# Two attentions and a routed mixture of experts on one core: logits in one block, the last tile emptied by two engines, a new order in the first two beats

## The chip, the cores and the metric

The kernel runs on one core of a Trainium2 chip. Its engines work side by side, each through its own queue in order: TensorE (PE; its weight loads are listed as PEld), VectorE (DVE), ScalarE (ACT), GpSimd (POOL), and SyncE (SP), which here issues nearly all DMA transfers. The metric is the device time of one execution in microseconds (us); smaller is better.

## The reference

```python
def sm_attn(qq, kk, vv):
    s = scale * np.matmul(qq, kk.transpose(0, 1, 3, 2))
    a = np.exp(s - np.max(s, axis=-1, keepdims=True))
    a = a / (np.sum(a, axis=-1, keepdims=True) + 1e-09)
    return np.matmul(a, vv)
p_packed = sm_attn(p, k, v)             # p: (8, 8, 32, 64); q, k, v: (8, 8, 576, 64)
out = sm_attn(q, p_packed, p_packed)    # attention back from the 32 packed rows
...
x = attn_out.transpose(0, 2, 1, 3).reshape(4608, 512)
logits = x @ w_gate                     # 8 experts
e_idx = np.argmax(logits, axis=1)
gate_w = softmax(logits)[row, e_idx]
eom = 1.0 / (1.0 + np.exp(-(x @ w_output_gate)))
for e in range(E):                      # only rows whose expert is e
    h = np.maximum(x[mask] @ w1[e], 0.0)        # 512 -> 1024
    out[mask] = gate_w[mask, None] * eom[mask, e, None] * (h @ w2[e])
```

## The kernel before

The eight batches are eight **beats**. A beat is the mixture of experts of one batch, `ffn(b)`: for each of two halves of its 576 rows (256 and 320) eight up-projections `ps_h` (6 matmuls each, since both factors are split into a high and a low part, `ah`/`al` and `Gh`/`Gl`), each followed by a relu on ACT and the remainder of the split on DVE, both into `hT`; and then the products `ps_o` with `w2h`/`w2l`, tile by tile of 128 rows (`L565`; the short last tile at `L580`), each scaled into `ob` and stored. One expert is guessed per batch (`estar`, from the mean of the packed rows), all rows go through that one, and rows that chose another are put right at the end (`leftover`).

`ffn` yields after each piece: 1 to 8 are the up-projections of the first half, 9 to 16 its products, 17 to 24 and 25 to 35 those of the second half. At yield i the characters of `PLANS[b]` behind `i:` each emit one more piece of other work, and this order is the order of every engine's queue (it is written by hand; no planner moves anything):

- `y` is the next piece of `encode` for the next batch (scores `ps_s`, maxima, exponentials, transposes `ps_a1T`, their copies `a1T`, product `ps_pp`, transpose `ps_ppT`, gate projections `ps_pg`, copied to `pg`, the guess `ps_e`/`e_top`/`estar`); `x` the same for the batch after it
- `t` is the next piece of `route` for the batch of this beat, `r` for the next batch (scores `ps_s2T`, softmax on DVE and ACT, transposed attention `a2T`, its parts `ah` and `al`, the logits, `gate`, the count `ps_cnt`, and last the update of `keys`)
- `W`/`w` weights (loads from the guessed expert's address, then casts `w2h` and remainders `w2l`), `G`/`g` the products `ps_G` of the packed rows with `w1` and their parts `Gh`/`Gl`, `k`, `v`, `q` loads, `d` delayed stores

`START` is the same for what comes before beat 0; a digit in it emits matmuls on zeros, `keep_warm`, as many as `CFG["warm"]` says. PSUM has 8 banks, four with the tag "a" (attention) and four with "f" (up-projections, products, logits, count). A piece that needs a bank waits in its engine's queue for the last reader of the bank's earlier content; a tile of SBUF is waited for in the same way (`ob` has four buffers).

The logits: `a2T` holds the transposed attention, 576 columns for each of NG = 2 halves of the features. Stationary is `pg`, the 16 gate columns written twice beside each other (32 columns); the four blocks of 128 columns of `a2T` go to four groups of 32 PSUM partitions, side by side, and the remaining 64 columns to the bank's columns 128 to 191. Both parts are copied by ACT, transposed by PE, and copied by DVE into `L`.

The last tile of the last beat (tile 3 of batch 7) is computed in two halves of 256 columns in two banks; DVE empties the first while PE computes the second, which ACT empties.

Of the kernel before, what the change touches and what calls it, by code (L numbers as in the profile page):

```python
# [18 lines left out]

P = 128  # L20
BANK = 512
CFG = dict(raw=6, rq=2, pa=4, w1=4, wst=4, w2=6, a1T=2, at=2, row=2, ht=4, ob=4, last=(4, 2, 3), warm=(8, 2, 2, 2, 2, 0, 5),
           pool=("w1.0", "w1.1", "w1.2", "w1.3", "w2.0", "w2.1", "w2.2", "w2.3", "w3.3", "w4.3", "w5.3", "w6.3", "w7.3",
                 "sub0.0.1", "al0.0.1"))


# [2 lines left out]
START = "kkvvqqkkYYYY1YY2YYY3YY4YYtYYWtttWYtttttttty6GGvvqqkkvv"  # L29
BESIDE = "8:ry 9:yrr 10:yrrrt 11:yr 12:wrr 13:wrqq 14:rkk 15:r "  # L30
REST = "16:xr 17:x 18:r 19:xvv 20:x 22:x 24:x 25:xxw 26:ww 27:rw 28:r 30:r 31:rxg 32:xg 33:gw 34:ww"
PLANS = ["2:GG 4:WW 6:W 8:WW 9:tt 10:tWW 11:yy 12:Wyy 13:tt 14:ttty 15:ty 16:tyy 17:ty 19:yt 20:y 21:ryyr 22:yr 23:y "
# [3 lines left out]
         "1:y 2:y 4:yWW 5:y 7:yy 8:ry 9:rry 10:rrry 11:ryw 12:rrw 13:rqq 14:rkkt 15:r " + REST] \  # L36
        + ["0:yW 1:y " + BESIDE + REST] * 3 \
        + ["0:yW 1:y " + BESIDE + REST.replace("16:xr", "20:r"), "0:W 8:l 18:l 20:lt 22:l 23:l 24:l 25:l 27:l 28:l 30:l"]
# [3 lines left out]
def tile_packed_attn_then_moe(ctx, tc, qT, kT, v, pT, w_go, w1, w2, out):  # L42
# [82 lines left out]
    wgo = const.tile([P, NPAIR, 2 * E], F32, name="wgo")  # L125
    L = const.tile([P, T, 2 * E], F32, name="L")
    nc.gpsimd.memset(L[REM:, TF], 0.0)
    oh = const.tile([P, T, E], F32, name="oh")
    nc.gpsimd.memset(oh[REM:, TF], 0.0)

# [81 lines left out]
    def encode(b):  # L212
# [87 lines left out]
        ps_g = [bank("ps_pg", "f" if b else "a")[:, :2 * E] for _ in range(NG)]  # L300
        by_head(ps_g, ppT, [wgo[:, c] for c in range(NPAIR)])
        yield
        R[b] = pg = sb.tile([P, NG, 2, 2 * E], F32, tag="pg", name="pg", bufs=3)
        for g in range(NG):
            nc.vector.tensor_copy(pg[:, g], ps_g[g].rearrange("p (i e) -> p i e", i=1).to_broadcast([P, 2, 2 * E]))
        yield
        if b:
            yield from guess(pg[:, :, 0, 0:E])

    def route(b):  # L310

        ah = sb.tile([P, NG, S], F32R, tag="ah", name="ah", bufs=CFG["at"], **WIDE)
        al = sb.tile([P, NG, S], F32R, tag="al", name="al", bufs=CFG["at"], **WIDE)
        A[b] = (ah, al)

        s2 = [scores(b, packed[b], pairs("q", b, hf), "s2T", "a" if b else "f") for hf in range(2)]
        yield
        both = sb.tile([P, NG, 2, HS], F32, tag="row", name="s2", bufs=CFG["row"])
        rows = [both[:, g] for g in range(NG)]

        def turn(hf):
            for g in range(NG):
                nc.vector.transpose(rows[g][:, hf], s2[hf][g])

        turn(0)
        yield
        if b:
            turn(1)
            yield
        for part in ([0, 1],) if b else ([0], [1]):  # L330
            ts = slice(part[0] * HS, (part[-1] + 1) * HS)
            n = (ts.stop - ts.start) // NP
            sf = [x.rearrange("p a b -> p (a b)")[:, ts] for x in rows]
            sv = [x.rearrange("p (j n) -> p j n", n=NP) for x in sf]
            sms = []
            for g in range(NG):
                mx = sb.tile([P, S // NP, 1], F32, tag="mx", name="mx", bufs=2)[:, :n]
                nc.vector.tensor_reduce(mx, sv[g], axis=AX.X, op=ALU.max)
                eng("sub", b, part[0], g).tensor_tensor(sv[g], sv[g], mx.to_broadcast([P, n, NP]), ALU.subtract)  # L339
                yield  # L340
            for g in range(NG):
                nc.scalar.activation(sf[g], sf[g], AF.Exp, scale=QK)  # L342
            yield
            if part == [0]:
                turn(1)
                yield
            for g in range(NG):
                sm = sb.tile([P, S // NP, 1], F32, tag="sm2", name="sm2", bufs=2)[:, :n]
                nc.vector.tensor_reduce(sm, sv[g], axis=AX.X, op=ALU.add)
                nc.vector.tensor_scalar_add(sm, sm, 1e-9)  # L350
                nc.vector.reciprocal(sm, sm)
                sms.append(sm)
                yield
            for g in range(NG):
                eng("mul", b, part[0], g).tensor_tensor(sv[g], sv[g], sms[g].to_broadcast([P, n, NP]), ALU.mult)
                nc.vector.transpose(a2T[:, g, ts], sf[g])  # L356
                if ts.stop == S:
                    nc.sync.dma_start(a2_d[b * T:(b + 1) * T, :, g].rearrange("t p n -> p t n"),
                                      a2T[:, g].rearrange("p (t n) -> p t n", n=P))
                yield  # L360
            for g in range(NG):
                nc.scalar.copy(ah[:, g, ts], a2T[:, g, ts])  # L362
            yield
            for g in range(NG):
                eng("al", b, part[0], g).tensor_tensor(al[:, g, ts], a2T[:, g, ts], f(ah[:, g, ts]), ALU.subtract)  # L365
            yield
        lgs = sb.tile([P, P + REM], F32, tag="row", name="lgs", bufs=CFG["row"])
        lg = bank("ps_lg", "f")
        pgs = R.pop(b).rearrange("p g i e -> p g (i e)")
        beside([lg[t_ * 4 * E:(t_ + 1) * 4 * E, :P] for t_ in range(TF)],  # L370
               [[(pgs[:, g], a2T[:, g, t_ * P:(t_ + 1) * P]) for g in range(NG)] for t_ in range(TF)])
        matmuls(lg[:4 * E, P:P + REM], [(pgs[:, g], a2T[:, g, SF:S]) for g in range(NG)])
        yield
        nc.scalar.copy(lgs[:, :P], lg[:, :P])
        nc.scalar.copy(lgs[:4 * E, P:], lg[:4 * E, P:P + REM])
        yield
        lT = bank("ps_lgT", "f")
        nc.tensor.transpose(lT[:, :P], lgs[:, :P], ident)
        nc.tensor.transpose(lT[:REM, P:P + 4 * E], lgs[:4 * E, P:], ident[:4 * E, :4 * E])
        yield  # L380
        nc.vector.tensor_copy(L[:, :TF], lT[:, :P].rearrange("p (t i e) -> p t i e", i=2, e=2 * E)[:, :, 0])
        nc.vector.tensor_copy(L[:REM, TF], lT[:REM, P:P + 2 * E])
        yield from gate(b)

    def gate(b):
# [152 lines left out]
    def store():  # L538

        while keep:  # L540
            b, t_, cs, ob, ps, sc, by_dve = keep.pop(0)
            if b < 2 and t_ < 2:
                nc.scalar.activation(ob, ob, AF.Copy, scale=sc)
            elif by_dve:
                nc.vector.tensor_scalar_mul(ob[:, cs], ps[:, cs], sc)
            else:
                nc.scalar.activation(ob[:, cs], ps[:, cs], AF.Copy, scale=sc)  # L547
            nc.sync.dma_start(out[b * S + t_ * P:b * S + (t_ + 1) * P, cs], ob[:, cs])

    def product_out(b, t_, c0, hs):  # L550
        w2s = W[b][1]
# [4 lines left out]
        sc = scm_all[:r, b, t_:t_ + 1]  # L556
        if t_ < TF:
            lo = 640 - 2 * P + c
            parts = 2 if (b, t_) == (B - 1, CFG["last"][-1]) else 1
            for x in range(parts):  # L560
                cs = slice(x * DM // parts, (x + 1) * DM // parts)
                ps = bank("ps_o", "f") if x else ps
                for fc in range(FC):
                    for i, (a, m) in enumerate(three((hs[fc][:, c:c + P], hs[fc][:, lo:lo + P]), w2s[fc])):
                        nc.tensor.matmul(ps[:, cs], a, m[:, cs], start=fc == i == 0, stop=fc == FC - 1 and i == 2)  # L565
                    if fc % 2 and (fc < FC - 1):
                        yield
                keep.append((b, t_, cs, ob, ps, sc, parts > 1 and x == 0))
                if b > 1 or t_ > 1:
                    store()  # L570
                else:
                    nc.scalar.copy(ob, ps)
        else:
            seq = []
            for fc in range(FC):
                wh, wl = w2s[fc]
                both, one = (hs[fc][:, c:c + 2 * r], wh, 2 * r), (hs[fc][:, c:c + r], wl, r)
                seq += [one, both] if fc == FC - 1 else [both, one]
            for i, (a, m, n) in enumerate(seq):
                nc.tensor.matmul(ps[:n], a, m, start=i == 0, stop=i == len(seq) - 1)  # L580
                if i % 6 == 5:
                    yield
            low = sb.tile([r, DM], F32, tag="ob", name="low", bufs=CFG["ob"])
            nc.scalar.copy(low, ps[r:2 * r])
            nc.vector.tensor_tensor(ob[:r], ps[:r], low, ALU.add)
            nc.vector.tensor_scalar_mul(ob[:r], ob[:r], sc)
            nc.sync.dma_start(out[b * S + SF:(b + 1) * S], ob[:r])
# [254 lines left out]
```

## Time and profile before

| | us |
|---|---|
| three runs | 416.25, 416.55, 418.04; median 416.55 |
| profiled execution | 416.11 |
| its span, first to last instruction | 414.3 |
| PE busy in the span | 399.4 |
| DVE, ACT, POOL busy | 282.4, 181.7, 41.1 |

The span is what the trace shows; the 1.8 us around it belong to the execution and are in no row. Busy time overlaps between engines; only waits of the engine that the others wait for lengthen the span.

### The profile page before, as it was taken

Reading aid. Unit: us, or ns where it says so; the run is one execution under the profiler, and the core shown is the slowest. Engines: PE = TensorE matmul, PEld = TensorE weight load, DVE = VectorE, ACT = ScalarE, POOL = GpSimd, SP = SyncE. Lnnn points to the kernel's source line nnn. Section 1 sums busy time; section 2 is a strip of 40 time slices with the busy share of each in tenths; the row PEclk is TensorE's granted clock in tenths of the full one; section 3 lists DMA queues with packets and bytes.
Section 4 is the critical chain, followed back from the end, with each engine's and each line's share of the span. In section 5 each row is a group of like instructions: output and inputs, shape, how many; then the busy total and the mean of one; then the engine's idle time right before and its main releaser. Section 6 shows DMA issues by size and latency. Waiting matters only on the chain.

```text
span 414.3 us, 9584 instructions
## 1 busy us (share of the span) xinstructions
PE 399.4 (96%) x3696; PEld 321.1 (78%) x3696; DVE 282.4 (68%) x817; ACT 181.7 (44%) x411; POOL 41.1 (10%) x36
## 2 busy tenths in 40 slices
PE   6899999899999999999999999999999999999994
PEld 4658876677768888788977888788877888798873
DVE  2669588684886876749774786749774795758620
ACT  2356425562467337442645337351645335532310
POOL 6010000360024200020002000020002000010010
PEclk9999999999999999999999999999999999999998
DMA  7899329930797089602992079701960058102911
GB/s 243 320 375 411 112 61 367 394 126 33 251 404 266 9 271 411 247 27 102 347 412 90 6 229 405 295 27 65 357 226 34 27 196 326 38 27 87 366 30 53
DMA packets 36687, 83.61 MB, mean 202 GB/s; under 512 B 3614, under 2 KB 16288, under 8 KB 36640
## 3 DMA queue, kind: packets, MB, share of 16 engines
q1 hardware_dynamic: 36608, 82.98, 54.2%
q8 instruction: 30, 0.49, 0.5%
q14 instruction: 17, 0.14, 0.1%
q0 software_dynamic: 32, 0.00, 0.0%
HBM read 67.76 MB, written 15.27 MB: 200 GB/s over the span
## 4 chain that ended last, share of the span: by engine, by line
PE 78%; DVE 1%; ACT 1%; issue 0%
PE ps_o L565 38%; PE ps_h L85 21%; PE ps_o L580 6%; PE ps_G L92 3%; PE ps_pp L92 2%; PE ps_s L92 2%; PE ps_s2T L92 2%; PE ps_a1T L240 1%; PE ps_lg L92 1%; ACT hT L523 1%; PE ps_lh L685 0%; PE ps_lo L685 0%; ACT a L231 0%; DVE Gl L77 0%; PE ps_lg L85 0%; DVE al L365 0%
## 5 line engine op out<-in xcount | busy, mean ns | idle before, releaser
L565 PE MATMUL ps_o<-w2h,hT 128*128 128x512 f32 (+1 forms) x528 | 168.5, 391 | 0.0
L565 PEld LDWEIGHTS ps_o<-w2h,hT 128*128 128x128 f32 x528 | 98.2, 188 | 25.8 <-ACT Gh L76 5.0
L526 DVE SCALAR_TENSOR_TENSOR hT<-ps_h,hT 128x256 fp32r<-128x256 f32 x192 | 61.0, 352 | 59.9 <-ACT hT L523 59.3
L565 PE MATMUL ps_o<-w2l,hT 128*128 128x512 f32 (+1 forms) x264 | 101.4, 384 | 0.0
L85 PE MATMUL ps_h<-ah,Gh 128*128 128x256 f32 (+1 forms) x256 | 78.3, 306 | 1.7 <-DVE hT L526 0.5
L85 PE MATMUL ps_h<-ah,Gl 128*128 128x256 f32 (+1 forms) x256 | 75.8, 296 | 0.0
L85 PE MATMUL ps_h<-al,Gh 128*128 128x256 f32 (+1 forms) x256 | 75.7, 296 | 0.0
L523 ACT ACTIVATE hT<-ps_h 128x320 fp32r<-128x320 f32 (+1 forms) x128 | 51.3, 414 | 43.4 <-PE ps_h L85 42.3
L463 POOL TENSOR_TENSOR w2l<-wst,w2h 128x1024 fp32r<-128x1024 f32 x13 | 31.2, 2407 | 308.6 <-ACT w2h L461 278.7
L565 PEld LDWEIGHTS ps_o<-w2l,hT 128*128 128x128 f32 x264 | 49.7, 188 | 8.6
L85 PEld LDWEIGHTS ps_h<-ah,Gh 128*128 128x128 f32 x256 | 48.5, 189 | 6.2 <-issue 1.8
L85 PEld LDWEIGHTS ps_h<-al,Gh 128*128 128x128 f32 x256 | 48.6, 190 | 0.2
L85 PEld LDWEIGHTS ps_h<-ah,Gl 128*128 128x128 f32 x256 | 48.5, 190 | 0.2 <-DVE Gl L77 0.2
L547 ACT ACTIVATE ob<-ps_o,scm_all 128x512 f32<-128x512 f32 (+1 forms) x28 | 19.0, 680 | 39.7 <-PE ps_o L565 37.1
L461 ACT CAST w2h<-wst 128x1024 fp32r<-128x1024 f32 x32 | 33.4, 1069 | 3.3 <-PE ps_o L565 2.8
L77 DVE TENSOR_TENSOR Gl<-ps_G,Gh 128x512 fp32r<-128x512 f32 (+1 forms) x36 | 20.5, 624 | 10.5 <-ACT Gh L76 10.3
L463 DVE TENSOR_TENSOR w2l<-wst,w2h 128x1024 fp32r<-128x1024 f32 x19 | 23.2, 1220 | 6.2 <-ACT w2h L461 6.2
L362 ACT CAST ah<-a2T 128x576 fp32r<-128x576 f32 (+1 forms) x18 | 11.2, 620 | 33.7 <-DVE a2T L356 33.7
L580 PE MATMUL ps_o<-w2h,hT 128*128 128x512 f32 x64 | 25.7, 401 | 0.1
L342 ACT ACTIVATE s<-s 128x576 f32<-128x576 f32 (+1 forms) x18 | 11.1, 629 | 29.8 <-DVE s L339 29.2
L580 PE MATMUL ps_o<-w2l,hT 128*64 128x512 f32 x64 | 23.9, 393 | 0.0
L76 ACT CAST Gh<-ps_G 128x512 fp32r<-128x512 f32 (+1 forms) x36 | 17.1, 548 | 9.4 <-PE ps_G L92 8.9
(182 smaller groups left out, 440.7 us busy)
## 6 DMA issues: line engine op xcount, KB each, us to landing
w<-in_w_dram SPq DMA_DIRECT2D x36, 512.0 KB, 5.7
wst<-in_w_dram SPq DMA_DIRECT2D x36, 512.0 KB, 8.7
vt<-in_v_dram SPq DMA_DIRECT2D x16, 640.0 KB, 9.0
k<-in_kT_dram SPq DMA_DIRECT2D x14, 576.0 KB, 10.5
q<-in_qT_dram SPq DMA_DIRECT2D x14, 576.0 KB, 10.2
out_dram<-ob SPq DMA_DIRECT2D x31, 256.0 KB, 3.3
a_d<-a2T SPq DMA_DIRECT2D x16, 320.0 KB, 8.0
out_dram<-ob SPq DMA_DIRECT2D x10, 128.0 KB, 5.3
```

The costliest lines, as they stand in the source:

```text
L76: (hi_eng or nc.scalar.copy)(hi, src)
L77: (lo_eng or nc.vector).tensor_tensor(lo, src, f(hi), ALU.subtract)
L85: res = nc.tensor.matmul(dst, a, m, start=j == 0, stop=j == len(seq) - 1)
L92: res = nc.tensor.matmul(dst, a, m, start=j == 0, stop=j == len(seqs[0]) - 1)
L362: nc.scalar.copy(ah[:, g, ts], a2T[:, g, ts])
L461: nc.scalar.copy(hi, st)
L463: eng("w", b, j).tensor_tensor(lo, st, f(hi), ALU.subtract)
L523: nc.scalar.activation(hT[:, :n], ps, AF.Relu)
L526: nc.vector.scalar_tensor_tensor(hT[:, d0:d0 + s1 - s0], ps[:, s0:s1], 0.0, f(hT[:, s0:s1]), op0=ALU.max, op1=ALU.subtract)
L547: nc.scalar.activation(ob[:, cs], ps[:, cs], AF.Copy, scale=sc)
L565: nc.tensor.matmul(ps[:, cs], a, m[:, cs], start=fc == i == 0, stop=fc == FC - 1 and i == 2)
L580: nc.tensor.matmul(ps[:n], a, m, start=i == 0, stop=i == len(seq) - 1)
```

## The change

The gate columns of a batch now lie between blocks of zeros in one of three tiles `pgs`, cleared once at the start, so that a window of 32 columns has them above or below 16 zero columns. The four blocks use one window; the 64 remaining columns use the other and are added into the second 16 partitions of the first group. One 128x128 copy and one transpose then do for all five. The last tile is computed in one bank over its full width; DVE scales its left half and ACT its right half, and SP and ACT each issue one store. The remainder `w1.3` (fourth chunk of w2 of batch 1) is no longer on POOL's list and is done by DVE. Two counts of `warm` are smaller. In `PLANS[0]` and `PLANS[1]` pieces stand at other places; their number is the same.

```diff
-CFG = dict(..., warm=(8, 2, 2, 2, 2, 0, 5),
-           pool=("w1.0", "w1.1", "w1.2", "w1.3", "w2.0", ...
+CFG = dict(..., warm=(5, 2, 2, 2, 2, 0, 4),
+           pool=("w1.0", "w1.1", "w1.2", "w2.0", ...
...
-PLANS = ["2:GG 4:WW 6:W 8:WW 9:tt 10:tWW 11:yy 12:Wyy 13:tt 14:ttty 15:ty 16:tyy 17:ty 19:yt 20:y 21:ryyr 22:yr 23:y "
-         "24:wt 25:wkkrr 26:tr 27:trr 28:drqq 29:r 30:t 31:g 32:gr 33:rg",
-         "0:ytWW 1:t 2:yWW 3:t 4:yWW 5:vv 6:y 7:y 8:ytWW 9:yytt 10:y 11:y 12:yd 13:y 14:ry 15:rry 16:yrr 17:ryw 18:w 19:qq 20:kk 21:r 22:r "
-         "24:rx 25:rx 26:rx 27:rxt 28:rxvv 29:rw 30:rw 31:grww 32:g 33:grrw 34:xw",
+PLANS = ["2:GG 4:WW 6:W 8:WW 9:tt 10:tWW 11:yy 12:Wyy 13:tt 14:yyttt 15:t 16:tyy 17:ty 19:yt 20:y 21:ryyr 22:yyr "
+         "24:wt 25:wkkrr 26:tr 27:rr 28:drqq 29:r 31:g 32:gr 33:rg 35:tt",
+         "0:tWW 1:t 2:yWW 3:ty 4:yWW 5:vv 6:y 7:y 8:ytW 9:yyW 10:yyt 11:yy 12:ryd 13:yrr 14:yyrr 15:w 16:r 17:tw 18:t 19:qq 20:kk 21:r 22:r "
+         "24:rx 25:rx 26:rx 27:rx 28:rxvv 29:rw 30:rw 31:grww 32:g 33:grrw 34:xw",
...
+    pgs = [const.tile([P, 2 * NG + 1, 2 * E], F32, name=f"pg{i}") for i in range(3)]
+    for pg in pgs:
+        nc.gpsimd.memset(pg, 0.0)
...
-        R[b] = pg = sb.tile([P, NG, 2, 2 * E], F32, tag="pg", name="pg", bufs=3)
+        R[b] = pg = pgs[b % 3]
         for g in range(NG):
-            nc.vector.tensor_copy(pg[:, g], ps_g[g].rearrange("p (i e) -> p i e", i=1).to_broadcast([P, 2, 2 * E]))
+            nc.vector.tensor_copy(pg[:, 2 * g + 1], ps_g[g])
...
-        lgs = sb.tile([P, P + REM], F32, tag="row", name="lgs", bufs=CFG["row"])
+        lgs = sb.tile([P, P], F32, tag="row", name="lgs", bufs=CFG["row"])
         lg = bank("ps_lg", "f")
-        pgs = R.pop(b).rearrange("p g i e -> p g (i e)")
-        beside([lg[t_ * 4 * E:(t_ + 1) * 4 * E, :P] for t_ in range(TF)],
-               [[(pgs[:, g], a2T[:, g, t_ * P:(t_ + 1) * P]) for g in range(NG)] for t_ in range(TF)])
-        matmuls(lg[:4 * E, P:P + REM], [(pgs[:, g], a2T[:, g, SF:S]) for g in range(NG)])
-        yield
-        nc.scalar.copy(lgs[:, :P], lg[:, :P])
-        nc.scalar.copy(lgs[:4 * E, P:], lg[:4 * E, P:P + REM])
+        pg = R.pop(b).rearrange("p i e -> p (i e)")
+        for g in range(NG):
+            up, down = slice(4 * E * g, 4 * E * (g + 1)), slice(4 * E * g + 2 * E, 4 * E * (g + 1) + 2 * E)
+            for t_ in range(TF):
+                nc.tensor.matmul(lg[t_ * 4 * E:(t_ + 1) * 4 * E, :P], pg[:, down], a2T[:, g, t_ * P:(t_ + 1) * P],
+                                 start=g == 0, stop=g == NG - 1 and t_ > 0)
+            nc.tensor.matmul(lg[:4 * E, :REM], pg[:, up], a2T[:, g, SF:S], start=False, stop=g == NG - 1)
+        yield
+        nc.scalar.copy(lgs, lg[:, :P])
         yield
         lT = bank("ps_lgT", "f")
-        nc.tensor.transpose(lT[:, :P], lgs[:, :P], ident)
-        nc.tensor.transpose(lT[:REM, P:P + 4 * E], lgs[:4 * E, P:], ident[:4 * E, :4 * E])
-        yield
-        nc.vector.tensor_copy(L[:, :TF], lT[:, :P].rearrange("p (t i e) -> p t i e", i=2, e=2 * E)[:, :, 0])
-        nc.vector.tensor_copy(L[:REM, TF], lT[:REM, P:P + 2 * E])
+        nc.tensor.transpose(lT[:, :P], lgs, ident)
+        yield
+        lv = lT[:, :P].rearrange("p (t i e) -> p t i e", i=2, e=2 * E)
+        nc.vector.tensor_copy(L[:, :TF], lv[:, :, 0])
+        nc.vector.tensor_copy(L[:REM, TF], lv[:REM, 0, 1])
...
-            parts = 2 if (b, t_) == (B - 1, CFG["last"][-1]) else 1
-            for x in range(parts):
-                cs = slice(x * DM // parts, (x + 1) * DM // parts)
-                ps = bank("ps_o", "f") if x else ps
...
+            if (b, t_) == (B - 1, CFG["last"][-1]):
+                rows = out[b * S + t_ * P:b * S + (t_ + 1) * P]
+                l, r_ = slice(0, DM // 2), slice(DM // 2, DM)
+                nc.vector.tensor_scalar_mul(ob[:, l], ps[:, l], sc)
+                nc.scalar.activation(ob[:, r_], ps[:, r_], AF.Copy, scale=sc)
+                nc.sync.dma_start(rows[:, l], ob[:, l])
+                nc.scalar.dma_start(rows[:, r_], ob[:, r_])
+            else:
+                keep.append((b, t_, ob, ps, sc))
```

## Rows read from the trace of the kernel before

**Rows 1.** Windows: us, busy us (instructions) by engine, granted PE clock, DMA share, GB/s.
```profile
0.00:20.00 20.00, 14.92 (x238) 10.39 (x238) 8.75 (x32) 5.21 (x14) 7.59 (x20) 1.00 0.80 277
...
66.89:69.20 2.31, 2.31 (x34) 0.59 (x33) 2.21 (x6) 2.17 (x4) 0.00 (x0) 1.00 1.03 420
...
74.87:78.79 3.92, 2.73 (x53) 1.18 (x52) 2.45 (x4) 1.62 (x2) 0.35 (x1) 1.00 1.07 397
...
178.76:225.80 47.04, 47.04 (x438) 38.54 (x437) 33.45 (x95) 22.14 (x50) 2.45 (x2) 1.00 0.57 211
```

**Rows 2.** Chain that ended last, in steady beats: start us, us, what.
```profile
197.06 1.13 PE ps_s L92 x32
198.19 0.57 PE ps_lg L92 x16
198.76 0.20 PE ps_lg L85 x4
...
210.99 0.15 PE ps_lgT L379
...
218.14 1.88 PE ps_G L92 x32
...
225.80 5.75 PE ps_h L85 x48
```

**Rows 3.** The same chain at the end of beat 0 and start of beat 1.
```profile
72.53 0.21 DVE g_cnt L430
...
73.59 1.20 DVE Gl L77 x2
74.79 1.33 DVE al L365 x2
...
76.77 1.31 PE ps_s L92 x16
```

**Rows 4.** Timeline of PE in beat 0: start us, us; idle before, releaser.
```profile
40.83 1.03 PE L240 MATMUL ps_a1T<-ident,a 128*128 128x128 f32 x8
...
46.03 0.65 PE L92 MATMUL ps_pp<-vt,a1T 128*32 128x64 f32 x32 [0.50 <-ACT a1T L246]
```

**Rows 5.** Timeline of DVE and SP's queue in beat 0, around the guess.
```profile
56.01 0.84 DVE L323 STREAM_TRANSPOSE s<-ps_s2T 128x288 f32<-128x288 f32 x2
...
57.22 0.15 DVE L290 COPY e_top<-ps_e 128x8 f32<-128x8 f32 x1
...
58.93 2.59 SPq L447 DMA_DIRECT2D w<-in_w_dram  x4
```

**Rows 6.** Timeline of ACT at the start of beat 1.
```profile
76.74 0.69 ACT L547 ACTIVATE ob<-ps_o,scm_all 128x512 f32<-128x512 f32 x1 [2.54 <-DMA out_dram<-ob]
77.33 1.04 ACT L461 CAST w2h<-wst 128x1024 fp32r<-128x1024 f32 x1
79.80 0.39 ACT L523 ACTIVATE hT<-ps_h 128x256 fp32r<-128x256 f32 x1 [1.44 <-PE ps_h L85]
```

**Rows 7.** DMA issues from 64 to 80 us: KB each, median us to landing.
```profile
out_dram<-ob SPq DMA_DIRECT2D x4, 256.0 KB, 7.5
```

**Rows 8.** Timeline of PE in the second half of beat 1.
```profile
103.97 0.39 PE L85 MATMUL ps_h<-ah,Gh 128*128 128x320 f32 x1 [0.33 <-DVE e_top L290]
```

**Rows 9.** Chain that ended last, in the last beat.
```profile
369.14 10.91 PE ps_o L565 x48
...
398.04 10.09 PE ps_o L565 x66
```

**Rows 10.** Timeline of DVE and ACT on the last tile.
```profile
405.28 0.48 DVE L545 TENSOR_SCALAR ob<-ps_o,scm_all 128x256 f32<-128x256 f32 x1 [6.82 <-PE ps_o L565]
...
408.15 0.47 ACT L547 ACTIVATE ob<-ps_o,scm_all 128x256 f32<-128x256 f32 x1 [5.01 <-PE ps_o L565]
```

**Rows 11.** Timeline of PE in the first microseconds.
```profile
1.12 3.78 PE L114 MATMUL warm<-blank 128*128 128x128 f32 x16 [1.12 <-DVE blank L106]
...
7.51 1.40 PE L92 MATMUL ps_s<-k,pt 64*32 64x288 f32 x16 [0.91 <-DMA k<-in_kT_dram]
```

More of the change, by code (lines that the diff above doesn't have):

```diff
@@ L21 @@
 BANK = 512
-CFG = dict(raw=6, rq=2, pa=4, w1=4, wst=4, w2=6, a1T=2, at=2, row=2, ht=4, ob=4, last=(4, 2, 3), warm=(8, 2, 2, 2, 2, 0, 5),
-           pool=("w1.0", "w1.1", "w1.2", "w1.3", "w2.0", "w2.1", "w2.2", "w2.3", "w3.3", "w4.3", "w5.3", "w6.3", "w7.3",
+CFG = dict(raw=6, rq=2, pa=4, w1=4, wst=4, w2=6, a1T=2, at=2, row=2, ht=4, ob=4, last=(4, 2, 3), warm=(5, 2, 2, 2, 2, 0, 4),
+           pool=("w1.0", "w1.1", "w1.2", "w2.0", "w2.1", "w2.2", "w2.3", "w3.3", "w4.3", "w5.3", "w6.3", "w7.3",
                  "sub0.0.1", "al0.0.1"))
@@ L302, in encode @@
         yield
-        R[b] = pg = sb.tile([P, NG, 2, 2 * E], F32, tag="pg", name="pg", bufs=3)
+        R[b] = pg = pgs[b % 3]
         for g in range(NG):
-            nc.vector.tensor_copy(pg[:, g], ps_g[g].rearrange("p (i e) -> p i e", i=1).to_broadcast([P, 2, 2 * E]))
+            nc.vector.tensor_copy(pg[:, 2 * g + 1], ps_g[g])
         yield
         if b:
-            yield from guess(pg[:, :, 0, 0:E])
+            yield from guess(pg[:, 1::2, 0:E])
     def route(b):
@@ L540, in store @@
         while keep:
[L541 to L548, printed above, removed]
+            b, t_, ob, ps, sc = keep.pop(0)
+            nc.scalar.activation(ob, ob if b < 2 and t_ < 2 else ps, AF.Copy, scale=sc)
+            nc.sync.dma_start(out[b * S + t_ * P:b * S + (t_ + 1) * P], ob)
     def product_out(b, t_, c0, hs):
@@ L558, in product_out @@
             lo = 640 - 2 * P + c
-            parts = 2 if (b, t_) == (B - 1, CFG["last"][-1]) else 1
-            for x in range(parts):
-                cs = slice(x * DM // parts, (x + 1) * DM // parts)
-                ps = bank("ps_o", "f") if x else ps
[L563 to L566, printed above, removed]
-                        yield
-                keep.append((b, t_, cs, ob, ps, sc, parts > 1 and x == 0))
+            for fc in range(FC):
+                for i, (a, m) in enumerate(three((hs[fc][:, c:c + P], hs[fc][:, lo:lo + P]), w2s[fc])):
+                    nc.tensor.matmul(ps, a, m, start=fc == i == 0, stop=fc == FC - 1 and i == 2)
+                if fc % 2 and (fc < FC - 1):
+                    yield
[8 more added lines that the diff above has]
+                keep.append((b, t_, ob, ps, sc))
                 if b > 1 or t_ > 1:
```

## The prediction

> **What bounds the kernel now.** I read the windows by stage first: in a steady beat the reader should see TensorE (PE) busy for every one of its 47.04 us [rows 1]. There, time is PE work and nothing else: an edit is worth the PE instructions that it takes away, and edits to DVE, ACT or POOL are worth nothing. Next I read the chain that ended last. In a steady beat it is one unbroken run of PE pieces, which gives the price of each piece when nothing waits [rows 2]; about the start of beat 1 it leaves PE, and the reader should see DVE pieces, and then a PE piece that costs more than in a steady beat [rows 3]. PE is late only in the first two beats, so what their new plan is worth is read from the waits there: rows 4 to 8. The last beat ends in one tile, its emptying and its store [rows 9, 10]; the first microseconds have filler matmuls [rows 11].
>
> **The change part by part.** The sum is made against the profiled execution, 416.11 us (span 414.3 and 1.8 around it); the median of the three runs is 416.55, 0.44 above it.
>
> *Logits.* Removed on PE: the second transpose, 0.15 in each beat [rows 2]. In beats 2 to 7 it lies on the path: 6 x 0.15 = 0.9 us off. (Beats 0 and 1 are counted with their waits below.) The logit matmuls stay ten instructions, recorded as 16 and 4; they took 0.57 + 0.20 = 0.77 [rows 2], four column groups side by side and then the remainder in the first group. Now the remainder follows each half, still in the first group, whose own work is unchanged. I take 0. Bounds: 0.20 less a beat if the remainder hides beside the other groups, 0.20 more if its return to the first group stops the queue: 8 x 0.20 = 1.6 either way. ACT loses a 32x64 copy and DVE writes smaller pg copies: hidden behind PE in a steady beat, 0. The three memsets are POOL work long before anything reads pg: 0.
>
> *Beat 0.* The a1T copies (the second y of 14) move ahead of the steps that write ah. The transposes that they copy ended by 41.9, yet PE stood 0.50 before ps_pp for these copies [rows 4], because they were behind the ah casts in ACT's queue. Moved up they fall where ACT waited for a2T: 0.5 off, bounds 0 and 0.5. What they pass, ah and al of the second half, is read only by the matmuls after ps_pp. Then the guess of the expert (y at 22, not 23) passes the second turn of the scores on DVE: it starts at 56.01 rather than 57.22, 1.2 us earlier, and with it the weight loads that wait for it in SP's queue [rows 5]. The turn and the hT pieces behind it come 1.0 later; what reads them last in that half is PE work still to come. The first reader of these weights, ps_G, took 2.31 us [rows 1] against 1.88 in a steady beat [rows 2]: 0.4 off if it waited for the loads. With the transpose: 0.5 + 0.4 + 0.15 = 1.05 off.
>
> *Start of beat 1.* Three edits meet here. The keys update (the last t, 73.59 - 72.53 = 1.06 us of DVE) goes behind Gl and al [rows 3]. The scores of batch 2 go behind two up-projections, so they no longer stand in PE's queue waiting for the banks that Gl frees. Logits and up-projection thereby move ahead of them. The stretch from 74.87 to 78.79 is 3.92 us [rows 1]; its work is ps_s 1.13 and logits 0.77 [rows 2], so 2.0 us is waiting. DVE's al then ends at 74.79 + 1.33 - 1.06 = 75.1, less what beat 0 gave, just as PE has finished the logits: the 2.0 can all go.
> What is late next is ACT. Its scaling of the last tile of beat 0 waited until 76.74 for a store that frees its buffer, and a 1.04 us cast and the first relu are queued behind it [rows 6]. That cost nothing, since PE came late anyway; after the cast ACT even stood idle 1.44. Now PE wants a bank for its fourth up-projection at 74.87 - 1.05 + 0.77 + 3 x 0.72 + 1.13 = 77.9 (0.72 is 5.75 / 8 [rows 2]), and the logit copy that frees it is done 0.69 + 1.04 + 0.39 and its own time, about 2.3, after the wait ends. If the store lands 1.2 earlier, as the loads ahead of it do, that is 77.8: no wait. If it lands as before, it is 79.0; and ACT's work up to the exponentials that the a1T transposes need then ends only 1.4 (its idle time) earlier, while PE comes 1.05 + 2.0 = 3.05 earlier: 1.7 given back. Bounds 0 and 1.7; I take 0.6, nearer to the first since the store, 7.5 us to landing [rows 7], queues behind those loads: 2.0 - 0.6 = 1.4 off.
>
> *Rest of beat 1.* The guess and the softmax of batch 2 move into DVE's gap ahead of the second half, and PE's wait of 0.33 for e_top goes [rows 8]. But the exponentials (r at 16) now stand before the first relu of that half on ACT, and count and keys come at 17 and 18, 1.06 us of DVE between two hT pieces. I take 0.2 off; bounds 0.5 off, 0.5 on. The fourth w2l of batch 1 goes from POOL to DVE, and is ready before PE's product comes to it: 0.
>
> *End.* 48 full-width records take 10.91, 0.227 each; the last 66, of which 18 are full and 48 of half width, take 10.09 [rows 9]. So the halved tile costs 10.09 - 18 x 0.227 = 6.0, and in one run 24 x 0.227 = 5.45: 0.55 off; I take 0.3, as the short runs about the last beat's leftover pieces are slower. Then both halves of one bank are read. Side by side that is one 0.48, as now; one after the other 0.48 + 0.47 [rows 10]. No row shows two engines in one bank at once; the nearest, relu on ACT and remainder on DVE of ps_h, run in turn. I take in turn: 0.47 - 0.3 = 0.2 on; bounds 0.5 off and 0.5 on, for the second queue's store too.
> [...]
>
> *Filler matmuls.* Three fewer at the start, one fewer later. The first eight end at 4.9, and the scores after them wait for k [rows 11]: 0.
>
> Sum: -0.9 - 1.05 - 1.4 - 0.2 + 0.2 = -3.35; 416.11 - 3.35 = 412.8. I forecast 412.7.
>
> **Rivals.** *All waits go.* The store lands early (0.6 not given back), the second half starts clean (0.3), the bank is read side by side (0.5), and some of the logit bound comes (0.4): 412.8 - 1.8 = 411. For it: DVE and PE have room in each place. Against: all must hold. Chance 0.2.
> *ACT keeps what beat 1 should win.* The store lands as late as before, 1.7 instead of 0.6 given back, and the relu behind the exponentials costs 0.5 instead of winning 0.2: 412.8 + 1.1 + 0.7 = 414.6. For it: DMA is full there [rows 1, 7]. Against: the loads ahead start earlier. Chance 0.14.
> *The logits get no shorter.* The remainder stops the queue, 0.20 a beat: 412.8 + 1.6 = 414.4. For it: the first column group is visited four times in ten matmuls, two of them back to back with itself. Against: it has the same columns to do. Chance 0.08.
> [...] Chance 0.06.
> [...]
>
> **How the numbers follow.** The forecast, 411.6 to 414, has 0.52. What a measurement of this kernel can tell from no change is 0.5%, 2.1 us: 414.5 against the median. Faster: 0.52 + 0.2, half of the logit rival (0.04) and a third of the ACT rival (0.05): 0.81. Same: the rest of those two, 0.13. Slower: 0.06. Range: below, the first rival with the rest of the logit bound, 410.2; above, the ACT rival with the end at its bound, 415.2; outside stay the slow start and the tails of the others. The forecast's own range is 411.6 to 414.
>
> **What would show it.** One lgT record of PE a beat, and beats 3 to 5 at 46.9; no PE wait before ps_pp in beat 0; the w loads of batch 1 issued at about 57; ps_h of beat 1 ahead of ps_s without a gap; on ACT, how long its last scaling of beat 0 waits for the store; at the end, DVE and ACT on ps_o one behind the other. The prediction is wrong if a steady beat does not shorten, if PE in the first half of beat 1 loses over 1.7 us to ACT, or if PE pieces before 20 us are longer than before.

## The result, and the profile after

The changed kernel took 411.69 us (median of four; 408.49 to 415.98) against 416.4 for the kernel before (median of four): ratio 0.987, 95% interval 0.9827 to 0.9913. It is 1.3% faster, and the interval leaves out 1; the prediction said 412.7, with 410.2 to 415.2. On a second chip it took 411.68 against 415.58, ratio 0.9894 (0.9857 to 0.993). The rows here are of the execution profiled there (409.46 to 412.71 over six runs, span 408.6), because the execution profiled first was the slow one of the four, 415.98, with a granted clock between 0.50 and 0.66 in several stretches of its first 36 us.

Where the time went is read from both traces cut at the same instructions of PE: the first up-projection `ps_h` of beat 0, the `ps_G` late in beat 0 and in beat 1, the `ps_G` in beat 6, and the end. View of windows (columns as in [rows 1]), kernel before:

```profile
0.00:23.80 23.80, 18.25 (x264) 11.89 (x264) 11.91 (x43) 6.45 (x18) 8.11 (x22) 1.00 0.82 290
23.80:66.89 43.09, 42.19 (x364) 33.57 (x364) 32.29 (x100) 21.39 (x54) 0.56 (x1) 1.00 0.66 239
66.89:121.38 54.49, 52.46 (x490) 39.75 (x489) 42.00 (x114) 27.45 (x65) 11.88 (x5) 1.00 0.66 253
121.38:355.77 234.39, 234.39 (x2145) 192.44 (x2144) 167.05 (x486) 109.88 (x240) 16.95 (x8) 1.00 0.54 198
355.77:414.30 58.53, 52.13 (x437) 43.48 (x436) 29.18 (x78) 16.50 (x36) 3.61 (x2) 0.98 0.29 104
```

The same, changed kernel:

```profile
0.00:26.27 26.27, 19.24 (x257) 11.76 (x257) 11.88 (x43) 6.55 (x18) 8.82 (x25) 1.00 0.78 275
26.27:66.62 40.35, 39.98 (x361) 33.11 (x361) 31.80 (x99) 20.93 (x52) 0.00 (x0) 1.00 0.70 256
66.62:118.75 52.13, 50.88 (x489) 39.71 (x488) 41.52 (x121) 27.64 (x64) 9.16 (x4) 1.00 0.75 285
118.75:351.46 232.71, 232.71 (x2141) 191.99 (x2140) 165.69 (x479) 109.37 (x234) 17.27 (x8) 1.00 0.53 194
351.46:408.60 57.14, 51.85 (x413) 42.10 (x412) 29.43 (x80) 16.70 (x37) 3.60 (x2) 0.98 0.30 106
```

The spans differ by 5.70: the start is 2.47 *longer*, beat 0 is 2.74 shorter, beat 1 2.36, the five beats behind it 1.68, the end 1.39. The sum of the prediction had 0, 1.05, 1.75 (start and rest of beat 1, with one transpose), 0.75 and -0.2 in these places. Every stretch behind the start gave more than forecast, and the start, which was put at nothing, took 2.5 back. These are two single executions: the medians on the second chip are 3.9 apart, and about 1.0 of beat 0's 2.74 is the profiled execution of before alone, as shown below.

The chain in a steady beat of the changed kernel answers [rows 2] (start us, us, what):

```profile
195.19 0.36 PE ps_lg L376 x8
195.55 0.04 PE ps_lg L378
195.58 0.27 PE ps_lg L376 x6
195.86 0.11 PE ps_lg L378 x2
...
207.89 0.11 PE ps_lgT L383
208.00 5.48 PE ps_o L561 x24
```

The four logit pieces make 0.78, the two of before 0.77: the forecast's 0. One `ps_lgT` is left. But the 24 products behind it take 5.48, where the kernel before needed 5.67 for the same 24 behind its second, narrow transpose:

```profile
210.88 0.11 PE ps_lgT L378
210.99 0.15 PE ps_lgT L379
211.13 5.67 PE ps_o L565 x24
```

So a beat gained 0.15 + 0.19 = 0.34. The window of a whole beat agrees, against 47.04 in [rows 1]:

```profile
168.10:214.80 46.70, 46.70 (x442) 38.44 (x448) 33.39 (x95) 22.05 (x48) 2.40 (x1) 1.00 0.57 211
```

### The profile page after: what moved, and what is told of

It reads as the page before. It is cut to its first block, busy times and chain, and to the rows that moved or that the text cites. A ratio compares the mean times of both kernels' runs of the same rounds, so it can differ in the third digit from the quotient of the medians.

```text
span 414.3 us, 9502 instructions
## 1 busy us (share of the span) xinstructions
PE 398.0 (96%) x3656; PEld 320.6 (77%) x3656; DVE 280.6 (68%) x818; ACT 181.1 (44%) x403; POOL 38.8 (9%) x38
## 4 chain that ended last, share of the span: by engine, by line
PE 86%; DMA 5%; DVE 4%; ACT 3%; issue 1%; SPq 0%; ACTq 0%
PE ps_o L561 40%; PE ps_h L85 23%; PE ps_o L584 6%; PE ps_G L92 4%; PE ps_pp L92 2%; PE ps_s L92 2%; DMA out_dram<-ob 2%; PE ps_s2T L92 2%; PE ps_a1T L243 2%; DMA w<-in_w_dram 2%; DMA k<-in_kT_dram 1%; PE ps_lg L376 1%; DVE hT L531 1%; PE warm L114 1%; ACT w2h L466 1%; ACT hT L528 1%
## 5 line engine op out<-in xcount | busy, mean ns | idle before, releaser
L561 PE MATMUL ps_o<-w2h,hT 128*128 128x512 f32 x512 | 167.4, 397 | 0.1
L561 PEld LDWEIGHTS ps_o<-w2h,hT 128*128 128x128 f32 x512 | 96.1, 188 | 26.9 <-ACT Gh L76 4.2
L561 PE MATMUL ps_o<-w2l,hT 128*128 128x512 f32 x256 | 99.9, 390 | 0.0
L85 PE MATMUL ps_h<-ah,Gh 128*128 128x256 f32 (+1 forms) x256 | 79.3, 310 | 2.0 <-DVE hT L531 1.0
L468 POOL TENSOR_TENSOR w2l<-wst,w2h 128x1024 fp32r<-128x1024 f32 x12 | 28.8, 2407 | 308.6 <-ACT w2h L466 308.6
L561 PEld LDWEIGHTS ps_o<-w2l,hT 128*128 128x128 f32 x256 | 48.2, 188 | 9.0
L547 ACT ACTIVATE ob<-ps_o,scm_all 128x512 f32<-128x512 f32 x27 | 18.5, 687 | 33.2 <-PE ps_o L561 31.8
L468 DVE TENSOR_TENSOR w2l<-wst,w2h 128x1024 fp32r<-128x1024 f32 x20 | 24.4, 1220 | 7.1 <-ACT w2h L466 7.1
L584 PE MATMUL ps_o<-w2h,hT 128*128 128x512 f32 x64 | 25.6, 401 | 0.0
```

The source lines that it names most:

```text
L85: res = nc.tensor.matmul(dst, a, m, start=j == 0, stop=j == len(seq) - 1)
L468: eng("w", b, j).tensor_tensor(lo, st, f(hi), ALU.subtract)
L547: nc.scalar.activation(ob, ob if b < 2 and t_ < 2 else ps, AF.Copy, scale=sc)
L561: nc.tensor.matmul(ps, a, m, start=fc == i == 0, stop=fc == FC - 1 and i == 2)
```

## The experiments

Each was timed in five rounds beside the kernel before on the same chip. A ratio is its time over that of the kernel before, with the 95% interval in brackets. The first four shared one chip. *Early pace* is the pace of the first fillers, 3.78 / 16 = 0.24 us each [rows 11]; *full pace* that of the same shape later, 1.03 / 8 = 0.13 [rows 4].

**The change again.**

> The changed kernel again, for a profile at the full clock. Sum of the prediction, with the logits at the 0.33 us a beat that the first profile of it shows (46.71 against 47.04): 0.33 x 6 + 1.05 + 1.4 + 0.2 - 0.2 = 4.4 us less, ratio about 0.989, if the first 40 us run at a granted clock of 1.00 as in the kernel before. Rival, the start at the early pace: the granted clock falls to 0.50 in parts of the first 36 us in some executions (0.83 and 0.74 in the first two stretches of 20 us of the first profile), beat 0 begins up to 6 us later, and the executions spread over several us.

Measured: 0.9894 (0.9857 to 0.993), and the rows above.

**Fillers back.** `warm=(8, 2, 2, 2, 2, 0, 5)` in the changed kernel.

> The changed kernel with the fillers of the kernel before (8 and 5 instead of 5 and 4). If the missing fillers are what lets the granted clock fall at the start, this one shows 1.00 in the first 40 us, its executions lie closer together and its median is lower than that of the changed kernel by 1 to 4 us. If the fillers do nothing, the two are equal within 0.3%. If five fillers win time where the clock holds, this one is slower by up to 0.7 us (three at 0.24).

Measured: 408.89 us (407.98 to 411.35) against the change's 411.68; ratio 0.9837 (0.9801 to 0.9872). The two intervals overlap; the medians are 2.8 apart. The first `ps_h` came at 23.23, the span was 406.5. The executions lie no closer together, 3.4 us against 3.3, and both profiled ones read 1.00 in the first 36 us; so what the fillers give does not show in that column.

**The plan alone.** Before with the new `PLANS` and without `"w1.3"` on POOL's list.

> The kernel before with only the new plans of beats 0 and 1 (and the fourth w2l of batch 1 on DVE). By the prediction's terms without the transposes: 0.9 in beat 0, 1.4 at the start of beat 1, 0.2 behind: 2.5 us less, ratio 0.994, and ps_h of beat 1 starts 3 us earlier than before against the last product of beat 0. If ACT's wait for the store keeps what beat 1 should win: 0.7 to 1.4 less, 0.997 to 0.998. If all waits go: 3.9 less, 0.991.

Measured: 0.9931 (0.9906 to 0.9956), 2.9 us less (1.8 to 3.9). Its windows between the cuts above: beat 0 41.21, beat 1 53.20, the five beats 234.39 as before.

**The logits alone.** Before with `pgs`, one copy and one transpose.

> The kernel before with only the new logits. If both the transpose (0.15) and the logit matmuls (0.77 to about 0.64) shorten, 8 x 0.29 to 0.33 = 2.3 to 2.6 us less, ratio 0.994, and the beats 3 to 5 are 46.71. By the prediction's step, the matmuls count as equal: 8 x 0.15 = 1.2 less, 0.997.

Measured: 0.9927 (0.9898 to 0.9956), 3.0 us less (1.8 to 4.2). Its five beats take 232.85 against 234.39; eight times 0.33 is 2.6. Its profiled execution had a granted clock of 0.82 from 8 to 12 us and 0.75 from 12 to 16, so its first stretches are not compared.

**The last tile alone** (the next four shared a chip). Before with the last tile in one bank over its full width, scaled by DVE and ACT, and stored from SP and ACT.

> The kernel before with the new last output tile and its two store queues alone; logits, plan and fillers as before. The sum of the prediction (0.2 us longer: 0.47 for the second engine behind the first, 0.3 back for one full-width run) gives a ratio of 1.0005. What the profiles of the first batch suggest (from PE's end to the end of the span 6.17 us in the kernel before, 5.57 and 5.75 in the two kernels that keep the halves, 5.1 in all three with the new tile; the run of PE itself 0.3 to 0.5 shorter) gives 0.6 to 1.5 us less, a ratio of 0.9965 to 0.9985. In the profile: DVE and ACT in turn on ps_o, 0.48 and 0.47, and both stores landing in under 2 us, where the single last one of the kernel before took about 3.

Measured: 414.54 against 415.41, ratio 0.9978 (0.995 to 1.0006): 0.9 less, 2.1 less to 0.25 more. The trace tells more than the times. Chain that ended last, and DMA issues (KB each, median us to landing), this kernel:

```profile
397.30 9.78 PE ps_o L556 x42
...
407.10 0.49 DVE ob L562
...
407.68 0.47 ACT ob L563
...
out_dram<-ob SPq DMA_DIRECT2D x1, 128.0 KB, 1.7
...
out_dram<-ob ACTq DMA_DIRECT2D x1, 128.0 KB, 1.7
```

PE's run is 10.09 - 9.78 = 0.31 shorter [rows 9], and DVE and ACT go in turn, as forecast. What the forecast lacked is the landing. The last store of the kernel before took 3.5:

```profile
out_dram<-ob SPq DMA_DIRECT2D x1, 128.0 KB, 3.5
```

From PE's last product to the end of the span it is 414.3 - 408.13 = 6.17 before and 412.1 - 407.08 = 5.02 here; the changed kernel has 5.07. The kernel with the plan alone, which keeps the halves, had 2.9 for that store and 5.57. This does not vary by luck: by the records of PE the stretch is 5.6 to 6.2 in all four profiled kernels with the halves and 5.1 in all ten with the new tile. Why the one store takes longer is not shown. In the kernel before, its equal on the same queue had been issued at 405.79 and had landed after 1.7, at 407.49, before the last one was issued at 408.65, so it did not wait behind that one.

**Fewer fillers alone.** The kernel before with `warm=(5, 2, 2, 2, 2, 0, 4)`.

> The kernel before with five and four filler matmuls in the place of eight and five; nothing else. Theory of the early pace: without the three fillers PE's work after the wait for k goes on at the early pace, as in the changed kernel, where restoring the fillers took 0.57 points off the ratio (2.8 us in the medians): a ratio of 1.003 to 1.009 here, a1T transposes near 11.6 us at about 0.21 each, and the first ps_h 2 to 3 us later. The prediction's step (fillers cost and give nothing): 1.000. If the loss comes only with the new plan, because it makes PE idle at the start in another way, 1.000 too.

Measured: 417.41 against 415.41, ratio 1.0047 (1.0026 to 1.0068), 2.0 us *slower* (1.1 to 2.8); first `ps_h` at 26.36, not 23.80. The loss belongs to the fillers and needs nothing of the new plan. The transposes are long, as that theory said:

```profile
11.07 1.92 PE L240 MATMUL ps_a1T<-ident,a 128*128 128x128 f32 x8
```

**A buffer for the last tile of beat 0**, with eight and five fillers.

```diff
-        ob = sb.tile([P, DM], F32, tag="ob", name="ob", bufs=CFG["ob"])
+        spare = b == 0 and t_ == TF
+        ob = sb.tile([P, DM], F32, tag="rq" if spare else "ob", name="ob", bufs=CFG["rq" if spare else "ob"], **(EVEN if spare else {}))
```

> The changed kernel with eight and five fillers, and with the last output tile of beat 0 in a buffer of its own, so that ACT's scaling of it needs no store to have landed. Theory of the late store (the prediction's: ACT waits for the store, and cast, relu and exponentials of the first half of beat 1 are late behind it): ACT's wait of 1.4 us is gone and with it PE's waits behind it in beat 1, 0.6 to 1.5 us less than the same kernel without the buffer (ratio 0.9837), so 0.980 to 0.982. Rival: PE waits there for DVE and for loads anyway, or only ACT gets earlier: the ratio stays within 0.001 of 0.9837.

Measured: 412.76 us, ratio 0.9925 (0.9902 to 0.9948): neither theory, but some 3.7 us slower than without the buffer (0.0088 of 415.4). ACT's wait for the store was gone, as meant. Timelines of DVE, POOL and PE and a window of PE's clock (columns as in [rows 1]) show what took its place:

```profile
75.62 0.31 DVE L435 TENSOR_SCALAR g_cnt<-ps_cnt 128x160 f32<-128x160 f32 x1
75.85 1.88 DVE L437 TENSOR_SCALAR g_ne<-iota,estar_all 128x8 f32<-128x8 f32 x1
77.77 2.42 DVE L439 TENSOR_TENSOR g_cnt<-g_cnt,g_ne 128x160 f32<-128x160 f32 x1
80.22 0.32 DVE L440 SCALAR_TENSOR_TENSOR keys<-g_cnt,keys 128x160 f32<-128x160 f32 x1
...
75.31 4.70 POOL L468 TENSOR_TENSOR w2l<-wst,w2h 128x1024 fp32r<-128x1024 f32 x2 [50.36 <-DMA out_dram<-ob]
...
80.94 0.39 PE L85 MATMUL ps_h<-ah,Gh 128*128 128x256 f32 x1 [2.80 <-DVE hT L531]
...
82.00:84.00 2.00, 2.00 (x11) 2.00 (x11) 1.39 (x5) 1.57 (x3) 0.18 (x1) 0.50 0.97 401
```

Two pieces of the count that take 0.22 and 0.32 in the other kernels end with the first and the second POOL instruction (2.35 each), 3.8 us late together; the piece that reads PSUM (`ps_cnt`) does not stretch (0.31). ACT's earlier cast had let POOL start early, at 75.31. `g_ne` ends at 77.73 and `g_cnt` at 80.19, POOL's pair at 77.66 and 80.01; why they end together is not shown.

The loss reaches PE as a wait of 2.80 for `hT`, 0.57 with eight fillers alone. Behind that wait the granted clock reads 0.50, and for some 3.4 us the `ps_h` records follow each other every 0.21 us, 0.12 before and after: about 1.5 us more. From `ps_G` late in beat 0 to `ps_pp` in beat 1 this kernel needs 25.26 us (65.89 to 91.15), with eight fillers alone 21.60 (64.20 to 85.80): the 3.7 lie here. The start of this execution was late as well, with the first `ps_h` at 25.03; that is another 1.8 us of its span.

**Twelve fillers**, and five later, in the changed kernel.

> The changed kernel with twelve fillers ahead of the first scores (and five later). If eight are enough, the four more end at the early pace at about 6.9 us, ahead of the wait for k, and the ratio is that with eight, 0.9837; if they delay the first scores, up to 0.9 us slower, 0.986. If more fillers make PE's full pace come earlier or more surely, 0.5 to 1.5 us faster, 0.980 to 0.9825, and the first scores and a1T transposes are shorter than with eight.

Measured: 409.51 us, 0.9859 (0.9835 to 0.9884): no better than eight. Here too one piece of the count met POOL (`keys`, 2.39, beside a POOL instruction from 74.80), and from `ps_G` to `ps_pp` it needs 22.11, 0.5 more than with eight. That is about half of the 0.9 us between the two ratios, so whether twelve without the meeting would differ from eight is not shown.

**The count back to its old place** (the next three shared a chip), with eight and five fillers; and the same with the spare buffer.

```diff
-         "24:wt 25:wkkrr 26:tr 27:rr 28:drqq 29:r 31:g 32:gr 33:rg 35:tt",
+         "24:wt 25:wkkrr 26:tr 27:trr 28:drqq 29:r 30:t 31:g 32:gr 33:rg",
```

> The changed kernel with eight and five fillers, and with the count and the keys update back where the kernel before has them (the steps t at 27 and 30, not both at 35): about 1.06 us of DVE ahead of Gl and al of the second half. Theory of the shared wait (shown so far by three profiles: a DVE piece of the count that starts beside POOL's w2l difference takes 1.9 to 2.4 us, as long as the POOL instruction lasts; with eight fillers the last piece ended 0.03 us before POOL began): the collision can't come, but al is 1.06 later, while PE waits there 0.58 for ACT behind the store: 0 to 0.6 us slower than with eight fillers alone, ratio 0.9837 to 0.985. The prediction's price of this move (with the scores' move 2.0 us of waiting removed): up to 1 us slower, 0.986.

Measured: 409.51 us, 0.9847 (0.98 to 0.9895). The count no longer meets POOL, and PE no longer waits for ACT's scaling behind the store.

> The same, and with the last output tile of beat 0 in a buffer of its own. If the buffer was slower (0.9925) because ACT's cast came earlier, POOL began earlier and two DVE pieces of the count then waited 1.7 and 2.1 us for POOL, that is gone here: the count takes 1.06 us in all, and the time is that of the kernel with eight fillers or up to 1 us less, a ratio of 0.981 to 0.985. If the buffer itself costs (its transfer delays the load that next uses the buffer) or the start of those runs was only disturbed by the clock, 0.989 to 0.993 again.

Measured: 409.09 us, 0.9833 (0.9798 to 0.9869). The buffer costs nothing once the count is out of POOL's way (0.9925 with it in the way), so the collision, with the clock behind it, was the cause. It gains nothing measurable either. From `ps_G` late in beat 0 to `ps_pp` in beat 1 PE needs 21.60 us with eight fillers alone (64.20 to 85.80), 21.54 with the count moved (66.40 to 87.94), and 21.53 with the buffer too (65.36 to 86.89): with the wait for the store gone, the same chain of relu, cast and exponentials on ACT still ends last ahead of `ps_pp`.

**Eight at the start, four later.** `warm=(8, 2, 2, 2, 2, 0, 4)`.

> The changed kernel with eight fillers at the start and four, not five, later. If the three at the start carry the loss, the ratio is that with both restored, 0.9837, and the first ps_h comes near 23.3 us; if the one later carries it, it is that of the change, 0.989, with a1T transposes near 11.6 us at 0.21 each and the first ps_h near 26.

Measured: 409.61 us, 0.9853 (0.982 to 0.9885); first `ps_h` at 22.64. The interval overlaps that of the change (0.9857 to 0.993), so the times alone do not decide; the traces point to the three at the start. Timelines of PE, first the change, then this kernel:

```profile
1.12 2.50 PE L114 MATMUL warm<-blank 128*128 128x128 f32 x10 [1.12 <-DVE blank L106]
...
5.59 1.18 PE L92 MATMUL ps_s<-k,pt 64*32 64x288 f32 x8 [0.42 <-DMA k<-in_kT_dram]
7.26 1.86 PE L92 MATMUL ps_s<-k,pt 64*32 64x288 f32 x16 [0.48 <-DMA k<-in_kT_dram]
10.62 1.22 PE L114 MATMUL warm<-blank 128*128 128x128 f32 x4 [1.50 <-ACT a L234]
11.63 1.92 PE L243 MATMUL ps_a1T<-ident,a 128*128 128x128 f32 x8
...
13.54 0.61 PE L114 MATMUL warm<-blank 128*128 128x128 f32 x4
```

```profile
1.12 3.78 PE L114 MATMUL warm<-blank 128*128 128x128 f32 x16 [1.12 <-DVE blank L106]
4.84 2.75 PE L92 MATMUL ps_s<-k,pt 64*32 64x288 f32 x32
9.09 0.71 PE L114 MATMUL warm<-blank 128*128 128x128 f32 x4 [1.50 <-ACT a L234]
9.64 0.75 PE L243 MATMUL ps_a1T<-ident,a 128*128 128x128 f32 x5
10.54 0.55 PE L243 MATMUL ps_a1T<-ident,a 128*128 128x128 f32 x3 [0.15 <-ACT a L234]
```

The reader should compare records of one shape: four filler records 1.22 against 0.71, 0.61 once the pace is full; transposes 1.92 for eight against 0.75 for five. In both kernels the granted clock reads 1.00 in every window here, so the column does not show it.

With eight fillers the full pace came more often, not always. Of the nine profiled executions with eight, six have short transposes, as here; in three (the logits alone, the buffer, and the count in its old place without the buffer) they take 1.91 to 1.92 for eight. All three profiled executions with five and none behind have them long. In the three with eight and long transposes the column does show it. The kernel with the buffer:

```profile
10.00:12.00 2.00, 1.91 (x9) 1.91 (x10) 0.00 (x0) 1.48 (x7) 0.00 (x0) 0.50 1.02 389
...
10.09 1.22 PE L114 MATMUL warm<-blank 128*128 128x128 f32 x4 [1.50 <-ACT a L234]
11.10 1.91 PE L243 MATMUL ps_a1T<-ident,a 128*128 128x128 f32 x8
```

PE had waited 1.50 for ACT, and the clock then reads 0.50. In the changed kernel, where the column reads 1.00, the same two pieces take 1.22 and 1.92: what is called the early pace here is the pace that the kernel with the buffer shows at a granted 0.50. The first `ps_h` comes at 22.64 to 24.09 in all executions with short transposes, twelve fillers and the next experiment included, and at 25.03 or later in all with long ones.

**Three fillers later.** Five at the start, three between the two halves of the first scores, five later.

```diff
-CFG = dict(..., warm=(5, 2, 2, 2, 2, 0, 4),
+CFG = dict(..., warm=(5, 2, 2, 2, 2, 0, 5, 3),
...
+        for hf in range(2):
+            if hf and not b:
+                keep_warm(7)
...
```

> The changed kernel with five fillers at the start, three more between the two halves of the first scores, where PE waits for k, and five later: as many fillers as in the kernel before, with three of them later. If what counts is that PE is not left idle in the wait for k, the full pace comes as with eight ahead (a1T transposes at 0.15 each, first ps_h near 23 us) and the ratio is 0.983 to 0.986. If it must be an unbroken run from the start, the pace stays early till about 13 us, the first ps_h comes near 26 us and the ratio is that of the change, 0.989 to 0.990.

Measured: 410.13 us, ratio 0.9866 (0.9824 to 0.9907), which overlaps both expectations. First `ps_h` at 24.02. Timeline of PE:

```profile
5.80 0.69 PE L92 MATMUL ps_s<-k,pt 64*32 64x288 f32 x8 [0.82 <-DMA k<-in_kT_dram]
6.42 0.94 PE L114 MATMUL warm<-blank 128*128 128x128 f32 x6
7.28 0.99 PE L92 MATMUL ps_s<-k,pt 64*32 64x288 f32 x16
...
10.33 0.75 PE L247 MATMUL ps_a1T<-ident,a 128*128 128x128 f32 x5
```

PE waits 0.82 for k and goes on at full pace: 0.69 for the eight scores at 5.80, 1.18 for the same eight in the changed kernel (at 5.59, above). But these scores run ahead of the three fillers at 6.42, and up to there PE's queue is that of the changed kernel. So the fillers did not bring this pace on, and it came with five ahead and a wait behind them; the first profile of the changed kernel has it too, 0.69 at 6.11 behind a wait of 1.15, and lost it again, with a granted clock of 0.55 from 8 to 10 us. Whether the three held the pace here, or this execution would have kept it without them, is not shown. What sets the pace there is not shown either.

## Why the prediction was right, step by step

**The total is right by errors that cancel.** The parts alone, with the ratio's interval turned into us:

| part | forecast | measured alone |
|---|---|---|
| logits, eight beats | -1.2 | -3.0 (-4.2 to -1.8) |
| plan of beats 0 and 1 | -2.5 | -2.9 (-3.9 to -1.8) |
| last tile | +0.2 | -0.9 (-2.1 to +0.25) |
| fewer fillers | 0 | +2.0 (+1.1 to +2.8) |

They add up to -4.8; the change as a whole took -4.4 (-5.9 to -2.9) on the second chip. (The forecasts here add up to -3.5, not -3.35: the sum of the prediction has seven transposes and lacks the one at 81.04 in beat 1.) Without the filler step it would have been 0.9837, -6.8.

**Filler matmuls, "0": this step failed.** It was argued that the scores behind the fillers wait for k anyway. True, but with five fillers the transposes behind that wait ran at the early pace (1.92 for eight) in all three profiled executions, with eight in three of nine. And what follows k is on the path: maxima, exponentials, transposes, the guess, and the address for the w loads, which go out at 18.75 us in the changed kernel, at 16.91 with eight and five fillers and at 16.25 with eight and four. The first `ps_h` came 26.27 - 23.23 = 3.0 later than with all fillers back. Not all of it stayed. With eight fillers PE catches up with the w loads (with eight and four its second `ps_G` took 1.77, in the changed kernel 1.09), so beat 0 gives back 40.97 - 40.35 = 0.6, and beat 1 gives back 0.27, since PE waits 0.58 for ACT there with eight fillers and 0.31 with five. What is left, 2.1, is the difference of the two spans, 408.6 and 406.5. One of the prediction's own signs of being wrong, that PE pieces before 20 us are longer than before, came true. No run shows the 0.06 that its sum of chances gives to slower; the runs showed the early pace at the start, at a cost of 2.0 us (fewer fillers alone), too little to make the change slower. The rows that spoke for it, 0.24 for a shape that later takes 0.13 [rows 4, 11], were in hand; what misled was to read the first wait for k as a cover for all that follows.

**Logits, 0.15 a beat: mis-sized, 0.34.** The matmuls were rightly put at 0. The missing 0.19 lies on both sides of the narrow transpose: in the timelines the 128-row transpose is followed by the narrow one of 32 rows after 0.20 us (210.72 to 210.92), and this one by the products after 0.14 (to 211.06). With the narrow one gone, the products follow the 128-row one after 0.02 (207.73 to 207.75). The chain, where ends are modelled, puts it all to the products: 5.48 behind a 128-row transpose, 5.67 or 5.68 behind the narrow transpose or `ps_G`. Why PE is later behind these is not shown.

**Beat 0, -1.05: right.** The profiled beat 0 of before was 43.09, but two kernels with the same plan (the last tile alone, fewer fillers alone) had 42.05 and 42.06, so about 1.0 of the 2.74 belongs to that execution. With eight fillers the changed beat 0 took 40.97: 1.08 less than those. (The plan alone: 41.21, 0.84 less, where 0.9 was forecast.) The wait ahead of `ps_pp` is gone. The w loads go out at 57.94 ("about 57" was forecast), but that is luck, for the beat began 2.5 later: counted from the beat's first `ps_h` they go out after 31.67, and after 34.15 and 34.14 in those two kernels, so 2.5 earlier where 1.2 was forecast.

**Start and rest of beat 1, -1.6: right in mechanism, near in size.** Timelines of ACT, PE and SP's queue, changed kernel, answer [rows 5, 6, 8]:

```profile
75.58 0.69 ACT L547 ACTIVATE ob<-ps_o,scm_all 128x512 f32<-128x512 f32 x1 [1.18 <-DMA out_dram<-ob]
...
76.31 0.39 PE L85 MATMUL ps_h<-ah,Gh 128*128 128x256 f32 x1 [0.31 <-ACT ob L547]
...
102.60 0.38 PE L85 MATMUL ps_h<-ah,Gh 128*128 128x320 f32 x1 [0.17 <-DVE hT L531]
...
57.94 2.59 SPq L452 DMA_DIRECT2D w<-in_w_dram  x4
```

The store lands 1.2 earlier (75.58 against 76.74; counted from `ps_G` late in beat 0, 8.96 against 9.85, 0.9 earlier). PE does wait for ACT behind it, 0.31 here and 0.58 with eight fillers, where 0.6 was taken, and the second half waits 0.17 in place of 0.33. One wait grew, which the forecast did not have: at 82.89 PE waits 0.58 for `hT`, 0.33 in the kernel before. The stretch is 2.36 shorter; the logits of two batches fall into it, 0.68, and the forecast's 1.6 with these makes 2.28. The plan alone gave 1.29. The store itself decides nothing: where it was taken out of ACT's way, and the count out of POOL's, ACT's own work ended last at the same place.

**End, +0.2: wrong sign by the traces.** The interval of the times, -2.1 to +0.25, still holds the forecast. The 0.3 of the one full-width run (0.31) and the 0.47 of the two engines in turn were right. The stores were taken as equal. The two of the new tile land in 1.7 each; the one that ended the span of before took 3.5 (2.9 in the kernel with the plan alone), for a reason that no run shows.

**Rivals.** That all waits go (411) is nearest in number, but not for its reasons: the engines run in turn at the bank (DVE from 407.10 for 0.49, ACT from 407.68, in the last tile alone). That the logits get no shorter fell with 46.70 a beat; that ACT keeps beat 1's gain fell with 0.31. The range was added up loosely: by its own terms the low end is 411 - (1.6 - 0.4) = 409.8 and the high end 414.6 + 0.3 = 414.9, and 411.7 lies inside either.

**The best version here** is the change with eight fillers: 0.9837 (five later, 408.89 us) and 0.9853 (four later). With the count in its old place and the spare buffer it is 0.9833; these are the same within what the runs can tell.

## What to carry to other kernels

Fillers in front of a wait are not free to remove because the wait hides them: three at the start and one later were worth 2.0 us here. Compare the pace of one instruction shape before and behind the wait, even where the granted clock reads 1.00 (four fillers took 1.22 and later 0.61 under that reading), and in more than one execution, since the pace at the start differed between them (three of nine with eight fillers had the early one). A long wait of PE cost more than its length: behind the 2.80 in beat 1 the granted clock read 0.50, and PE took another 1.5. Price a removed PE piece with its successor: without the narrow transpose, 0.15, the products behind it took 0.19 less as well. Before making one engine earlier, look what its follower will run beside: here an ACT wait removed made POOL early and DVE 3.8 us late.

## What was not expected of the hardware

DVE pieces that read and write SBUF ended only as a POOL instruction on SBUF ended (0.22 became 1.88, 0.32 became 2.42). Two executions differ there by tenths of a microsecond in the starts: `keys` took 0.33 where it started 0.09 before POOL (the changed kernel, 77.18 and 77.27), and 2.39 where it started 0.30 behind POOL (twelve fillers, 75.10 and 74.80). Stores of the same 128 KB at the end of the kernel landed after 1.7 us, one each on SP and ACT, and after 2.9 to 3.5 as the second of two on SP, though the first had landed before the second was issued. The clock column read 1.00 over 13 us in which PE's records ran at about half their later pace (four fillers 1.22 at 10.62, 0.61 at 13.54), the pace that they have in the kernel with the buffer at a granted clock of 0.50 (1.22).
